# Two chained attention blocks on one core: the layer norm's statistics are aggregated on GpSimd instead of VectorE for later tiles, and six of the planner's numbers move

## The chip, the cores and the metric

The kernel runs on one core of one Trainium2 chip. The metric is the device time of one launch in microseconds (us), as the median of several runs. A core has five engines with instruction streams of their own: TensorE (PE, matmuls into PSUM), VectorE (DVE), ScalarE (ACT), GpSimd (POOL) and SyncE (SP, which here only issues DMAs). Each runs its stream in order; an instruction that needs another engine's result waits for a semaphore, and all that stands behind it on the same engine waits with it.

## The reference

The input x has 2048 rows of 512 numbers. Four layers follow each other, each on the layer norm of x and added back to x:

```python
x = x + _A_ref(_layernorm(x), wq, wk, wv, wo)    # layer 0: softmax attention, 32 heads of 16, one key/value head
x = x + _B_ref(_layernorm(x), wqkv, wo)          # layer 1: linear attention with phi(t) = t+1 or exp(t)
x = x + _A_ref(...)                              # layer 2, weights of layer 0
x = x + _B_ref(...)                              # layer 3, weights of layer 1
```

The layer norm takes, per row, the mean m and the variance v over 512 numbers and gives (x - m) / sqrt(v + 1e-5). The attention of a layer A needs 32 x 2048 x 2048 exponentials; that is the bulk of the kernel.

## The kernel before, in words

The rows are cut into 16 tiles of 128. Everything stays in SBUF; only the inputs come in and x goes out.

**The order is planned, not written.** A small list scheduler (class Planner, L36) is run while the kernel is built. Each operation is handed to `op` (L87) with the engines that may do it, a duration that the author gave it in us, a priority (low goes first), a latency until its result may be used, and what it reads and writes. The planner plays the engines forward in time and notes the order in which it gave work to each; `finalize` (L328) and `emit` (L351) then write one instruction stream per engine in that order with the waits that the data needs. What the planner thinks of durations thus decides only the order; on the chip each engine goes through its list and waits where the plan was too hopeful. GpSimd's own results are waited for by semaphore too, even on GpSimd.

**Layers A (`run_a`, L956).** The scores are cut into 4096 blocks of 128 keys by 512 (four heads-by-queries groups side by side) in the two A layers together. TensorE makes the scores of a block (L965). The exponential is then done in one of two ways. ScalarE takes two or three blocks in one activation (L1150). Or VectorE does one block: L1247 writes an integer whose bits, read as bfloat16, are about the exponential, and three shifted copies of four such blocks at a time (L1289) are made, so that the weighted sum of four shifted versions comes close to the true exponential; TensorE then multiplies four versions instead of one (L1019). Which block goes to which engine is decided while planning: VectorE gets a block when its queue of planned work is short (`dve_split`, `dve_open`, `alone`, L1231 to L1266, with the bounds BLS, BLO, BLT and DXB), and near the end of an attention only while more than ENDL blocks are left (L1201). VectorE starts on blocks only once the keys of tile 11 are planned (KGATE). L1312 and L1314 take the sums out of PSUM, L1334 to L1345 normalise them, `epilogue` (L1351) projects and adds to x.

**Filling TensorE.** When TensorE has nothing to do, `fill` (L1045) gives it matmuls with zeros (L1064), as many columns as a credit allows, which grows by WORK / 3.413 columns per us and falls by the columns run (`work`, L146).

**Layers B (`run_b`, L1413)** are short. Layer 1's tiles 0 to 14 are normalised and projected while layer 0's exponentials still run, as each tile's x is ready; so are layer 3's during layer 2. Only tile 15 and what depends on all of them come after. Layer 2's first tiles start when layer 1's first x tiles are there.

**The calm flag.** `pl.calm` is False while an attention's exponentials are planned (set at L1085) and True in the kernel's first moments and between the attentions (L692, L1168). Some rules hold in only one of the two: LAG (L64) holds back an operation in calm times when a more urgent one is about to come, HTOL (L72) lets a matmul go ahead of the next scores if it makes them late by no more than that.

**The layer norm of a tile (`ln_tile`, L787)** is what the change touches:

- L793, VectorE: bn_stats over the 512 numbers of each row. For even and odd elements apart it gives count, mean and sum of squared deviations: six numbers, tile st.
- L794, VectorE: bn_aggr makes mean and variance of them, tile mv.
- `slow_rs` (L781): L782 adds 1e-5 to the variance (on VectorE when the flag is calm or the tile is below 4 or from 12 on, else on GpSimd), and L784, on GpSimd, raises it to the power -0.5, tile rs. For the few critical tiles (tile 0 of layer 0, tiles 0 and 1 of layer 2, tile 15 of layers 1 and 3) ScalarE does it instead (L797, L798).
- L802, VectorE: (x - mean) * rs, tile xn, one of six buffers.
- Then xn is transposed into xnT, either by a DMA on SP's queue (L719) or on TensorE (L822) with a copy out of PSUM by ScalarE or VectorE (L827, recorded as L705). In layers 1 and 3 tiles below FARB take the DMA.

On VectorE, L802 has a priority that puts it behind L1247 of blocks but ahead of the shifts of L1289.

Of the kernel before, what the change touches and what calls it, by code (L numbers as in the profile page):

```python
# [7 lines left out]
FP32 = mybir.dt.float32  # L8
I16 = mybir.dt.int16
ACTF = mybir.ActivationFunctionType  # L10
ALU = mybir.AluOpType

PE, AC, DV, PO, SP = "pe", "act", "dve", "pool", "sp"
ENGS = (PE, AC, DV, PO, SP)

P = 128
S, D, H, DH = 2048, 512, 32, 16
T = S // P
# [388 lines left out]
NBQ = 3  # L407
LAG = 0.18
LAGP = 0.05
# [5 lines left out]
ECRIT = (15,)  # L415
WORK = 5500
RING = 24
# [5 lines left out]
FARA = (4, 4)  # L423
FARB = 12
FARO = 12
# [3 lines left out]
BLO = 5.0  # L429
DXB = 1.4  # L430
BLT = 2.5
# [14 lines left out]
SHIFT = 64.0  # L446
ENDL = 12
NSH = 4
# [31 lines left out]
ACRS = True  # L480
# [3 lines left out]
KSP = True  # L484
HTOL = 0.02
HK = 0.3
MCOP = (DV,)*4
EVP = 1.2
# [8 lines left out]
def bass_interleave_layers__grouped_kv_mqa__linear_attn_block__prompt_kernel(  # L497
# [35 lines left out]
    mv = sb("mv", [P, T, 2], FP32)  # L533
    ve = sb("ve", [P, T], FP32)
    zs = sb("zs", [P, 4], FP32)
    rs = sb("rs", [P, T], FP32)
# [244 lines left out]
    def slow_rs(t, prio, quick):  # L781
# [3 lines left out]
           reads=[("ve", t), "mhalf"], writes=[("rs", t)], prio=prio - 9.0)  # L785

    def ln_tile(t, prio, far=False, crit=False, dtl=None):  # L787
        if t in two:
            two.discard(t)
            n = 2  # L790
        else:
            n = 1
            op({DV: (0.6, lambda e: e.bn_stats(st[:, t, 0, :], x_sb[:, t, :]))}, reads=[("x", t)], writes=[("st", t)], prio=prio, lat=0.13)  # L793
        op({DV: (0.09, lambda e: e.bn_aggr(mv[:, t, :], st[:, t, 0:n, :]))}, reads=[("st", t)], writes=[("mv", t)], prio=prio, lat=0.13)  # L794
        quick = pl.calm or t < QUICK[0] or t >= QUICK[1]
        if crit and ACRS:
            op({AC: (0.2, lambda e: e.activation(ve[:, t:t + 1], mv[:, t, 1:2], ACTF.Ln, bias=eps5[:]))}, reads=[("mv", t), "eps5"], writes=[("ve", t)], prio=prio, lat=0.12)  # L797
            op({AC: (0.2, lambda e: e.activation(rs[:, t:t + 1], ve[:, t:t + 1], ACTF.Exp, scale=-0.5))}, reads=[("ve", t)], writes=[("rs", t)], prio=prio, lat=0.12)  # L798
        else:
            slow_rs(t, prio, quick)  # L800
        i = yield ("acq", xn_pool, prio)
        op({DV: (0.325, lambda e: e.tensor_scalar(out=xn[:, i, :], in0=x_sb[:, t, :], scalar1=mv[:, t, 0:1], scalar2=rs[:, t:t + 1],  # L802
                                                op0=ALU.subtract, op1=ALU.mult))},
           reads=[("x", t), ("mv", t), ("rs", t)], writes=[("xn", i)], prio=prio, port=True)
        if far:
# [1076 lines left out]
```

## Time and profile before

| | |
|---|---|
| median of 3 runs | 1488.83 us (1487.35 to 1489.05) |
| the profiled execution's own time | 1489.33 us |
| its span, first to last instruction | 1487.6 us |
| around the span | 1.7 us |
| granted TensorE clock, mean | 0.999 |
| instructions of the layer norm's statistics on VectorE (L793, L794) | 60 and 64 |

The page's first two parts, busy time by engine and the span in 40 slices (each digit a share in tenths):

```profile
PE 1433.2 (96%) x14825; PEld 520.1 (35%) x14924; DVE 1439.2 (97%) x2686; ACT 1452.5 (98%) x1444; POOL 77.0 (5%) x155
...
PE   8999999999999999999999999999999999999998
PEld 5423333333333333333733333333333333333335
DVE  8999999999999999999878999999999999999996
ACT  8999999999999999999799999999999999999996
POOL 5000000000000000000011000000000000000000
```

How to read it: PE's busy time counts the filler matmuls. A row of a group of instructions gives line, engine, operation, output and inputs, shape, count, then busy time and mean duration in ns, then the engine's idle time ahead of them. Rows of the timeline give start and duration in us, and in brackets the idle time before and what ended it. Rows of windows give the stretch, its length, and the busy time of PE, PEld, DVE, ACT and POOL, each with its number of instructions, then granted clock, share of the DMA engines and GB/s.

### The profile page before, as it was taken

The page shows a single profiled execution, that of the slowest core. Times are in us where ns is not written, and L with a number is a line of the kernel's source. Part 1 is how long each engine was busy: PE and PEld are TensorE (multiplying, and loading weights), DVE is VectorE, ACT ScalarE, POOL GpSimd, SP SyncE. Part 2 cuts the span into 40 slices and gives each one's busy share as a digit, 9 for nine tenths or more (in the row PEclk, how much of TensorE's full clock was granted, in tenths as well). Part 3 has the DMA queues.
Part 4 walks back from the last instruction along what each step waited for, and adds up shares of the span by engine and source line. Part 5 has one row for each costly group of instructions (what it writes and reads, how often), then busy time and mean ns, then how long its engine had stood idle before and what let it go on. Part 6 is the DMA issues. An engine that isn't in the chain of part 4 may idle for free.

```text
span 1487.6 us, 36547 instructions
## 1 busy us (share of the span) xinstructions
PE 1433.2 (96%) x14825; PEld 520.1 (35%) x14924; DVE 1439.2 (97%) x2686; ACT 1452.5 (98%) x1444; POOL 77.0 (5%) x155
## 2 busy tenths in 40 slices
PE   8999999999999999999999999999999999999998
PEld 5423333333333333333733333333333333333335
DVE  8999999999999999999878999999999999999996
ACT  8999999999999999999799999999999999999996
POOL 5000000000000000000011000000000000000000
PEclk9999999999999999999999999999999999999999
DMA  5200000000000000000031000000000000000001
GB/s 115 72 9 9 9 8 7 6 7 6 9 9 9 9 5 5 2 2 2 2 47 40 2 12 9 12 9 5 8 9 5 9 9 9 9 2 2 2 2 58
DMA packets 53542, 20.74 MB, mean 14 GB/s; under 512 B 47232, under 2 KB 52864, under 8 KB 53376
## 3 DMA queue, kind: packets, MB, share of 16 engines
q1 hardware_dynamic: 52320, 18.36, 5.7%
q8 instruction: 120, 1.97, 0.6%
q14 instruction: 46, 0.38, 0.1%
q10 hardware_dynamic: 1056, 0.03, 0.0%
HBM read 5.28 MB, written 2.10 MB: 5 GB/s over the span
## 4 chain that ended last, share of the span: by engine, by line
DVE 46%; PE 38%; ACT 7%; issue 7%; DMA 1%; POOL 0%; POOLq 0%; SPq 0%; ACTq 0%
DVE FB L1247 22%; DVE FB L1289 16%; PE ps L1019 13%; PE ps L965 11%; ACT PT L1150 7%; PE ps L711 5%; PE ps L1064 4%; PE ps L879 2%; PE ps L1334 1%; DVE sacc L1312 1%; DVE st L793 1%; DVE xn L802 1%; DVE QT L1422 1%; DVE Osb L1345 1%; DVE sacc L1422 1%
## 5 line engine op out<-in xcount | busy, mean ns | idle before, releaser
L1150 ACT ACTIVATE PT<-ps 128x1024 bf16<-128x1024 f32 (+1 forms) x1309 | 1400.1, 1309 | 5.6 <-PE ps L1019 2.7
L1247 DVE TENSOR_SCALAR FB<-ps 128x512 int16<-128x512 f32 x1047 | 689.0, 680 | 4.4 <-PE ps L965 3.1
L965 PE MATMUL ps<-QT,KM 32*128 32x512 bf16 x4096 | 525.6, 385 | 24.9 <-ACT PT L1150 16.9
L1019 PE MATMUL ps<-FB,VW 128*32 128x512 bf16 x4188 | 526.1, 384 | 8.3 <-DVE sacc L1312 5.3
L1289 DVE TENSOR_SCALAR FB<-FB 128x2048 int16<-128x2048 int16 (+1 forms) x789 | 517.6, 676 | 0.3
L1019 PE MATMUL ps<-PT,V 128*32 128x512 bf16 x3049 | 472.8, 386 | 0.4 <-issue 0.3
L965 PEld LDWEIGHTS ps<-QT,KM 32*128 32x128 bf16 x4096 | 133.0, 91 | 466.5 <-ACT PT L1150 381.7
L1064 PE MATMUL ps<-QT,V 128*32 128x512 bf16 (+6 forms) x927 | 249.8, 347 | 0.4
L1019 PEld LDWEIGHTS ps<-FB,VW 128*32 128x32 bf16 x4188 | 130.4, 94 | 163.3 <-issue 97.1
L1019 PEld LDWEIGHTS ps<-PT,V 128*32 128x32 bf16 x3049 | 114.7, 94 | 102.9 <-issue 74.5
L1064 PEld LDWEIGHTS ps<-QT,V 128*32 128x32 bf16 x927 | 79.8, 96 | 88.6 <-issue 32.9
L784 POOL TENSOR_TENSOR rs<-ve,mhalf 128x1 f32<-128x1 f32 x59 | 43.9, 745 | 578.9 <-DVE ve L782 576.6
L711 PE MATMUL ps<-wqkv,xnT 128*128 128x512 bf16 (+1 forms) x217 | 62.2, 367 | 7.0 <-issue 3.5
L1419 ACT ACTIVATE phE<-ps 128x512 bf16<-128x512 f32 (+1 forms) x66 | 45.8, 696 | 6.0 <-PE ps L879 5.0
L782 POOL TENSOR_SCALAR ve<-mv 128x1 f32<-128x1 f32 x32 | 14.9, 466 | 683.8 <-DVE mv L794 683.7
L1312 DVE COPY sacc<-ps 128x512 f32<-128x512 f32 x64 | 43.6, 681 | 3.3 <-PE ps L1019 3.2
L1334 PE MATMUL ps<-identF,sacc 128*128 128x128 f32 x256 | 46.3, 291 | 0.0
L793 DVE BATCH_NORM_STATS2 st<-x_sb 128x6 f32<-128x512 bf16 x60 | 40.5, 681 | 2.5 <-DMA x_sb<-in_A_x_dram 2.3
L879 PE MATMUL ps<-xnT,wqkv 128*128 128x128 bf16 x512 | 38.0, 220 | 0.0
L879 PE MATMUL ps<-xnT,wq 128*128 128x128 bf16 x464 | 35.2, 220 | 0.0
L1334 PEld LDWEIGHTS ps<-identF,sacc 128*128 128x128 f32 x256 | 27.3, 140 | 20.6 <-issue 11.8
L879 PEld LDWEIGHTS ps<-xnT,wqkv 128*128 128x128 bf16 x512 | 29.5, 98 | 9.8 <-issue 7.0
(139 smaller groups left out, 630.4 us busy)
## 6 DMA issues: line engine op xcount, KB each, us to landing
out_dram<-x_sb SPq DMA_DIRECT2D x16, 128.0 KB, 1.7
x_sb<-in_A_x_dram SPq DMA_DIRECT2D x6, 256.0 KB, 5.0
wqkv<-in_B_wqkv_dram SPq DMA_DIRECT2D x1, 1536.0 KB, 8.7
xnT<-xn SPq DMA_TRANSPOSE x48, 2.4
x_sb<-in_A_x_dram SPq DMA_DIRECT2D x4, 128.0 KB, 2.4
wq<-in_A_wq_dram SPq DMA_DIRECT2D x1, 512.0 KB, 4.5
wo<-in_A_wo_dram SPq DMA_DIRECT2D x1, 512.0 KB, 5.4
wo<-in_B_wo_dram SPq DMA_DIRECT2D x1, 512.0 KB, 9.4
```

The lines of the kernel that those rows point to most:

```text
L711: return e.matmul(dst, lhsT=l, rhs=r, start=(k == 0), stop=(k == len(pairs) - 1))
L793: op({DV: (0.6, lambda e: e.bn_stats(st[:, t, 0, :], x_sb[:, t, :]))}, reads=[("x", t)], writes=[("st", t)], prio=prio, lat=0.13)
L879: ins = e.matmul(dst[:, g * P:(g + 1) * P], lhsT=lhs(g, k), rhs=rhs(k), start=(k == 0), stop=(k == FT - 1))
L965: return e.matmul(bank(b), lhsT=KM[r, sg.par, kt * P:(kt + 1) * P], rhs=QT[r, sg.t, :], start=True, stop=True)
L1019: ins = e.matmul(ps[32 * j:32 * j + 32, ACC * 512:(ACC + 1) * 512], lhsT=V[:, kt, :] if w is None else VW[:, kt, w, :], rhs=ap, start=(k = ...
L1064: o = op({PE: (n / 2400.0, lambda e: e.matmul(ps[32 * j:32 * j + 32, b * 512:b * 512 + n], lhsT=V0[:], rhs=QT[:, sg.t, 0:n], start=st, sto ...
L1150: ex = op({AC: (EXO + 0.4267 * n, lambda e, n=n, s_=s_, p_=p_: e.activation(PT[:, p_, 0:n * 512], ps[:, s_ * 512:(s_ + n) * 512], ACTF.Exp ...
L1247: o = op({DV: (0.602, lambda e: e.tensor_scalar(out=dst.bitcast(I16), in0=bank(b), scalar1=VB, scalar2=VLO, op0=ALU.add, op1=ALU.max))}, w ...
L1289: o = op({en: (du, lambda e, w=w, g_=g_: e.tensor_scalar(out=FB[:, g_, 0:n].bitcast(I16), in0=FB[:, f_, 0:n].bitcast(I16), scalar1=float(w ...
L1312: o = op({DV: (0.6, lambda e, src=src: e.tensor_copy(src, bank(ACC)))}, writes=[B_(ACC), key], prio=0.0, lat=0.15)
L1334: o = op({PE: (0.12, lambda e, c=c: e.transpose(ps[:, b * 512 + c * P:b * 512 + (c + 1) * P], src[:, c * P:(c + 1) * P], identF[:]))}, rea ...
L1419: op({AC: (0.07 + n / 1200.0, lambda e: e.activation(phE[:, i, 0:n], bank(b, n), ACTF.Exp))}, reads=[B_(b)], writes=[("phE", i)], prio=pr ...
```

## The change

In `ln_tile`, tiles from 4 on (PAT) whose statistics come from one bn_stats over the whole row, which are not critical, and which come up while the calm flag is down, no longer run bn_aggr on VectorE. GpSimd makes mean and variance from the six numbers of bn_stats in four operations on one column (half the difference of the two means d, the mean of the two sums w, the mean of the two means, d * d + w), then adds 1e-5 in a fifth and raises to the power -0.5 as before. For tiles 12 and up this takes the add of 1e-5 from VectorE too. The planner is told 0.3 us (PAD) for each. A way to run L802 on GpSimd as well is written but off (PXN is False). Six numbers of the planner move: LAG, WORK, FARB, DXB, ENDL and HTOL.

```diff
-LAG = 0.18
+LAG = 0.15
...
-WORK = 5500
+WORK = 5000
...
-FARB = 12
+FARB = 11
...
-DXB = 1.4
+DXB = 1.6
...
-ENDL = 12
+ENDL = 14
...
-HTOL = 0.02
+HTOL = 0.05
 HK = 0.3
+PAT = 4
+PAD = 0.3
+PXN = False
...
+    dm = sb("dm", [P, T, 2], FP32)
...
+    def pool_rs(t, prio):
+        a, b = st[:, t, 0, 0:3], st[:, t, 0, 3:6]
+        d, w = dm[:, t, 0:1], dm[:, t, 1:2]
+
+        def po(out, in0, s1, s2, op0, op1, reads, writes):
+            op({PO: (PAD, lambda e: e.tensor_scalar(out=out, in0=in0, scalar1=s1, scalar2=s2, op0=op0, op1=op1))}, reads=reads, writes=writes, prio=prio - 9.0)
+        po(d, a[:, 1:2], b[:, 1:2], 0.5, ALU.subtract, ALU.mult, [("st", t)], [("dm", t)])
+        po(w, a[:, 2:3], b[:, 2:3], 1.0 / D, ALU.add, ALU.mult, [("st", t)], [("dw", t)])
+        po(mv[:, t, 0:1], a[:, 1:2], b[:, 1:2], 0.5, ALU.add, ALU.mult, [("st", t)], [("mv", t)])
+        po(ve[:, t:t + 1], d, d, w, ALU.mult, ALU.add, [("dm", t), ("dw", t)], [("ve", t)])
+        op({PO: (PAD, lambda e: e.tensor_scalar(out=ve[:, t:t + 1], in0=ve[:, t:t + 1], scalar1=1e-5, scalar2=None, op0=ALU.add))},
+           writes=[("ve", t)], prio=prio - 9.0)
+        op({PO: (0.55, lambda e: e.tensor_tensor(out=rs[:, t:t + 1], in0=ve[:, t:t + 1], in1=mhalf[:], op=ALU.pow))},
+           reads=[("ve", t), "mhalf"], writes=[("rs", t)], prio=prio - 9.0)
+
     def ln_tile(t, prio, far=False, crit=False, dtl=None):
...
-        op({DV: (0.09, lambda e: e.bn_aggr(mv[:, t, :], st[:, t, 0:n, :]))}, reads=[("st", t)], writes=[("mv", t)], prio=prio, lat=0.13)
+        slow = n == 1 and not pl.calm and not crit and t >= PAT
+        if not slow:
+            op({DV: (0.09, lambda e: e.bn_aggr(mv[:, t, :], st[:, t, 0:n, :]))}, reads=[("st", t)], writes=[("mv", t)], prio=prio, lat=0.13)
         quick = pl.calm or t < QUICK[0] or t >= QUICK[1]
-        if crit and ACRS:
+        if slow:
+            pool_rs(t, prio)
+        elif crit and ACRS:
...
-        op({DV: (0.325, lambda e: e.tensor_scalar(out=xn[:, i, :], in0=x_sb[:, t, :], scalar1=mv[:, t, 0:1], scalar2=rs[:, t:t + 1],
+        op({(PO if slow and PXN else DV): (0.7 if slow and PXN else 0.325, lambda e: e.tensor_scalar(out=xn[:, i, :], in0=x_sb[:, t, :], scalar1=mv[:, t, 0:1], scalar2=rs[:, t:t + 1],
                                                 op0=ALU.subtract, op1=ALU.mult))},
-           reads=[("x", t), ("mv", t), ("rs", t)], writes=[("xn", i)], prio=prio, port=True)
+           reads=[("x", t), ("mv", t), ("rs", t)], writes=[("xn", i)], prio=prio - 9.0 if slow and PXN else prio, port=True)
```

## Prediction

> **What bounds the kernel now.** The first view is the page: its costliest groups. The reader is to see that two engines share one job, the 4096 blocks (128x512) of exponentials: ScalarE does 3049 of them (the count of matmuls that read its tile PT), VectorE 1047 (the count of L1247), and each of VectorE's costs a further share of the 789 shift operations of L1289.
>
> ```profile
> span 1487.6 us, 36547 instructions
> ...
> L1150 ACT ACTIVATE PT<-ps 128x1024 bf16<-128x1024 f32 (+1 forms) x1309 | 1400.1, 1309 | 5.6 <-PE ps L1019 2.7
> L1247 DVE TENSOR_SCALAR FB<-ps 128x512 int16<-128x512 f32 x1047 | 689.0, 680 | 4.4 <-PE ps L965 3.1
> ...
> L1289 DVE TENSOR_SCALAR FB<-FB 128x2048 int16<-128x2048 int16 (+1 forms) x789 | 517.6, 676 | 0.3
> L1019 PE MATMUL ps<-PT,V 128*32 128x512 bf16 x3049 | 472.8, 386 | 0.4 <-issue 0.3
> ```
>
> The second view is the busy time by stage (columns: PE, weight loads, VectorE, ScalarE, GpSimd, then the granted TensorE clock). In the two attention stretches both engines are full: VectorE is idle 3.6 us of 662 and 2.8 us of 629, ScalarE 0.8 and 1.9. GpSimd is nearly empty there. In the start, the middle and the tail there are holes on both.
>
> ```profile
> 0.00:43.00 43.00, 38.09 (x397) 21.19 (x401) 33.93 (x104) 36.89 (x41) 21.85 (x71) 1.00 0.57 143
> 43.00:705.00 662.00, 640.21 (x6584) 211.75 (x6626) 658.39 (x1176) 661.23 (x637) 21.28 (x23) 1.00 0.03 7
> 705.00:816.00 111.00, 107.77 (x1101) 53.54 (x1108) 90.14 (x213) 98.92 (x118) 15.65 (x37) 0.98 0.17 30
> 816.00:1445.00 629.00, 608.69 (x6368) 209.72 (x6405) 626.24 (x1129) 627.10 (x614) 18.22 (x24) 1.00 0.04 7
> 1445.00:1488.00 43.00, 38.41 (x387) 23.93 (x389) 30.50 (x68) 28.34 (x38) 0.00 (x0) 1.00 0.15 50
> ```
>
> So the bound is ScalarE and VectorE together, and time freed on one is worth only its share. The third view, VectorE's timeline, gives VectorE's real price: durations overlap, and the step from one start to the next is 0.60 us where the duration says 0.68.
>
> ```profile
> 297.74 0.68 DVE L1247 TENSOR_SCALAR FB<-ps 128x512 int16<-128x512 f32 x1
> 298.34 0.68 DVE L1289 TENSOR_SCALAR FB<-FB 128x2048 int16<-128x2048 int16 x1
> 298.94 1.40 DVE L1247 TENSOR_SCALAR FB<-ps 128x512 int16<-128x512 f32 x2
> ```
>
> A block costs ScalarE 1400.1 / 3049 = 0.459 us and VectorE 0.60 + 789 x 0.60 / 1047 = 1.052 us. If the planner hands blocks over until both end together, 1 us freed on VectorE shortens a stretch by 0.459 / (0.459 + 1.052) = **0.304 us**. That is the exchange rate of every VectorE term below; without a hand-over it would be nothing.
>
> **The change part by part.** *Relief of VectorE.* The views of lines L794 and L782:
>
> ```profile
> L794 DVE BATCH_NORM_AGGREGATE mv<-st x64: 125/171/209, 3.8 to 1458.0; 128x2 f32<-128x6 f32 x60, 128x2 f32<-128x12 f32 x4
> L782 POOL TENSOR_SCALAR ve<-mv x32: 208/397/1172, 12.2 to 1295.8; 128x1 f32<-128x1 f32 x32
> L782 DVE TENSOR_SCALAR ve<-mv x27: 97/144/153, 7.2 to 1424.9; 128x1 f32<-128x1 f32 x27
> ```
>
> The 32 adds on GpSimd are tiles 4 to 11 of all four layers, so the "calm" flag is down for them in every layer, the first and third too. Tiles from 4 on then take the new path in layers 0 and 2 (12 each) and, without the critical tile 15, in layers 1 and 3 (11 each): 46 aggregates leave VectorE, and with them the 14 adds of tiles 12 and up (4 + 3 + 4 + 3 of the 27). The steps are in this stretch of VectorE's timeline: aggregate to next start 0.09 us, add to next start 0.06 us.
>
> ```profile
> 95.75 0.17 DVE L794 BATCH_NORM_AGGREGATE mv<-st 128x2 f32<-128x6 f32 x1
> 95.84 0.66 DVE L1289 TENSOR_SCALAR FB<-FB 128x2048 int16<-128x2048 int16 x1
> 96.42 0.14 DVE L782 TENSOR_SCALAR ve<-mv 128x1 f32<-128x1 f32 x1
> 96.48 1.28 DVE L1289 TENSOR_SCALAR FB<-FB 128x2048 int16<-128x2048 int16 x2
> ```
>
> 46 x 0.09 + 14 x 0.06 = 5.0 us of VectorE, at 0.304 = **-1.5 us**. Bounds: by full durations 46 x 0.171 + 14 x 0.144 = 9.9 us, so -3.0; counting only the 22 tiles inside the full stretches (22 x 0.09 + 6 x 0.06 = 2.3 us), -0.7.
>
> *GpSimd's chain and the instruction behind it.* GpSimd now runs five small operations and the power per tile: four more instructions for 32 tiles, five more for 14, 198 in all. The instruction that waits for the last is L802 on VectorE; VectorE runs in order, so every L1247 and L1289 behind it waits too, and ScalarE's partner work with them. How GpSimd fares against VectorE is seen at one tile (VectorE first, then GpSimd):
>
> ```profile
> 385.27 0.68 DVE L793 BATCH_NORM_STATS2 st<-x_sb 128x6 f32<-128x512 bf16 x1
> 385.87 0.67 DVE L1247 TENSOR_SCALAR FB<-ps 128x512 int16<-128x512 f32 x1
> 386.46 0.17 DVE L794 BATCH_NORM_AGGREGATE mv<-st 128x2 f32<-128x6 f32 x1
> 386.55 1.26 DVE L1289 TENSOR_SCALAR FB<-FB 128x2048 int16<-128x2048 int16 x2
> 387.75 0.69 DVE L1247 TENSOR_SCALAR FB<-ps 128x512 int16<-128x512 f32 x1
> 388.54 0.41 DVE L802 TENSOR_SCALAR xn<-x_sb,mv,rs 128x512 bf16<-128x512 bf16 x1
> ```
>
> ```profile
> 386.72 1.13 POOL L782 TENSOR_SCALAR ve<-mv 128x1 f32<-128x1 f32 x1 [40.22 <-DVE mv L794]
> 387.93 0.57 POOL L784 TENSOR_TENSOR rs<-ve,mhalf 128x1 f32<-128x1 f32 x1
> ```
>
> An add on one column takes 1.13 us here because it ends only 0.1 us after the second L1289; at the start, with no L1289 about, the same add takes 0.23 us and the next instruction starts 0.16 us after it:
>
> ```profile
> 12.24 0.23 POOL L782 TENSOR_SCALAR ve<-mv 128x1 f32<-128x1 f32 x1
> 12.40 0.19 POOL L682 MEMSET ones<- 1x128 bf16 x1
> ```
>
> And L802 started 0.04 us after the power's end (388.50), about 0.2 us later than the 0.60 step from 387.75 allows: VectorE already waits a little. Now the walk for the new path at this tile. The statistics end at 385.95; GpSimd starts about 386.03 and gets two operations done before the pair of L1289 (from 386.46, since the aggregate is gone, to 387.66); the third ends near 387.8, the square-and-add near 388.1, the add of 1e-5 near 388.3, the power 0.57 later: about 388.95, which is 3.0 us after the statistics. The planner allows 0.13 + 5 small operations of 0.30 with two gaps of 0.08, then 0.55 + 0.08: 2.42 us (before: 0.13 + 0.09 + 0.13 + 0.58 + 0.63 = 1.56). So L802 is placed some 0.9 us later than before and the chain ends some 0.4 us later, relative to it, than before. The wait added lies between 0 (other work placed ahead of L802) and 1.2 us (a tile with two L1289 in the chain's way). I take 0.2 us, near the wait the row shows today, for the 22 tiles inside the full stretches: 4.4 us less some 1.3 us of such waits that go (7 tiles like this one, an estimate), 3 us, at 0.304 = **+0.9 us** (bounds 0 and 22 x 1.2 x 0.304 = +8.0).
>
> Does GpSimd hold VectorE? At the tile of 297 us the power is stretched, not the L1289 at 298.34, which starts in the middle of it and keeps its 0.68 us:
>
> ```profile
> 297.33 0.57 POOL L782 TENSOR_SCALAR ve<-mv 128x1 f32<-128x1 f32 x1 [39.06 <-DVE mv L794]
> 297.99 1.07 POOL L784 TENSOR_TENSOR rs<-ve,mhalf 128x1 f32<-128x1 f32 x1
> ```
>
> So nothing is added for it. (The Trainium skill, "SBUF — State Buffer", section "SBUF: two separate sides", says the two engines share a port pair as an exclusive lock that goes to whichever starts first, the other blocking fully. By that rule the L1289 would have waited here; the trace agrees that one blocks the other, but not that the first comer wins.)
>
> *Start and middle.* 24 tiles of layers 0 and 2 get a chain longer by four or five steps of 0.16 to 0.23 us, 0.6 to 1.2 us. GpSimd has room (21.85 of 43 us busy; 12 tiles add 52 instructions, 8 to 12 us). These delays overlap from tile to tile, and what they feed is the keys before VectorE's first block. If they reach it in full, VectorE loses 1 us twice, +0.6; nothing if hidden. I take **+0.2**.
>
> *FARB 12 to 11.* Tile 11 of layers 1 and 3 is transposed on TensorE, with a copy, and not by DMA (48 transposes of xn become 46 on SP's queue, which frees nothing that the end waits for). The copy:
>
> ```profile
> L705 DVE COPY xnT<-ps 128x512 bf16<-128x512 bf16 x10 | 4.1, 410 | 1.1 <-PE ps L822 1.1
> ```
>
> Two copies of 0.41 less the 0.08 overlap, 0.7 us, at 0.304: **+0.2** (0 to +0.3).
>
> *The planner's other numbers.* DXB 1.4 to 1.6 lets a block start on VectorE with more work before it; VectorE's idle time in the two stretches is 6.4 us, and I let 40% of it be filled, at 0.304: **-0.8** (0 to -1.9). WORK 5500 to 5000 gives the filler matmuls of L1064 less credit, LAG and HTOL move the order of the calm phases and of TensorE, ENDL stops VectorE's blocks two earlier at the end. TensorE is not late for ScalarE in the stretches (5.6 us of idle time before 1309 exponentials), so I take **0**; but one clock dip shows what order can cost, in the middle stretch (first its window, then ScalarE's timeline after it):
>
> ```profile
> 750.00:755.00 5.00, 4.37 (x33) 1.60 (x33) 2.85 (x6) 4.64 (x5) 0.00 (x0) 0.78 0.38 79
> ```
>
> ```profile
> 755.29 2.36 ACT L1150 ACTIVATE PT<-ps 128x1536 bf16<-128x1536 f32 x2 [0.65 <-PE ps L965]
> 757.88 1.45 ACT L1150 ACTIVATE PT<-ps 128x1536 bf16<-128x1536 f32 x1 [0.22 <-PE ps L965]
> 759.92 1.02 ACT L1150 ACTIVATE PT<-ps 128x1024 bf16<-128x1024 f32 x1 [0.59 <-PE ps L1019]
> ```
>
> Each dip costs ScalarE up to 0.65 + 0.22 + 0.59 = 1.5 us, so one gone or one more is 1.5 us either way. A changed order also moves the hand-over at each attention's end by a block of VectorE, 1.05 us, twice: about 2 us either way.
>
> Sum: -1.5 + 0.9 + 0.2 + 0.2 - 0.8 = **-1.0 us**. The profiled execution took 1489.33 us (span 1487.6 and 1.7 around it), so 1488.3 for its like; it lies 0.5 us above the median 1488.83. I forecast the median: **1487.8 us**.
>
> **The rivals.** *B, faster: the order comes out well.* Relief nearly in full (-2.5), no added waits, VectorE's idle time filled (-1.5), the dip gone (-1.5), the start no later, the copies +0.2: -5.3, 1483.5. For it: GpSimd's idle time in the stretches, and a longer planned chain that gives L802 more cover. Against it: each item is an upper bound. *C, slower: L802 stands in VectorE's queue.* The chain passes pairs of L1289 at most tiles and VectorE waits 1.2 us at 22 tiles: 26 us, +8.0 with a relief of only 1.5 against it, 1495.3. It decides from a mean wait of (3 + 1.5) / 0.304 / 22 = 0.67 us. For it: L802 starts 0.04 us after the power today. Against it: the planner counts the longer chain. *D, more clock dips:* with less filler three more of them at 1.5 us, +4.5, 1493.3; against it, the clock is 1.00 in both stretches. *E, GpSimd holds VectorE:* 198 instructions x 0.22 us x the share of L1289 in VectorE's busy time (517.6 of 1439, 0.36) = 15.7 us, +4.8, 1493.6; the row at 297.99 speaks against it. (This is what the rule of the Trainium skill's "SBUF — State Buffer", named above, would make of it.) *F, the change doesn't do what it says:* the aggregates stay where the calm flag is up, or nothing is handed over: 1488.8.
>
> **How the numbers follow.** 0.2% is 3 us, about what a measurement of this kernel can tell from no change. A (the sum, within 1485.9 to 1491.8) has 0.40, F 0.03: within 0.2% together 0.43. B has 0.35, faster. C 0.15, D 0.05, E 0.02: slower 0.22. For 8 in 10 I leave out some 0.07 of B below 1480 and 0.10 of C, D and E above 1494: range 1480 to 1494; the likeliest case alone 1485.9 to 1491.8.
>
> **What would show it.** Relief: 18 aggregates and 13 adds left on VectorE, and a few more L1247 (5 us / 1.51 = 3 more). Chain: from the end of the statistics to the power's end some 3 us in the stretches, and idle time ahead of L802 of about 4 us in all; over 15 us there is C. Dips: the granted clock by stage. E: L1289 longer than 0.68 us beside GpSimd. I am wrong if the middle or the tail changes by over 2 us, which nothing above prices, or if ScalarE's instruction mix (two or three banks) shifts.

## The result and the profile after

The changed kernel takes 1492.54 us (median of 7 runs, 1490.99 to 1494.05) against 1489.05 us (7 runs, 1487.35 to 1489.53): ratio 1.0026, interval 1.0016 to 1.0036. It is slower by a quarter of a per cent, 3.5 us. The range held the time; the forecast, 1487.8, was on the wrong side. The slow end of the range stood there for the rivals C, D and E, none of which is what the runs show, so that it held is luck.

Within one kernel the times fall into steps by the mean granted TensorE clock. The traces show what a step is: a profiled execution with no dip of the clock is at 1.000 (e12, e13), one with a single dip like that at 750 us is at 0.999 (before, after). Before, over the 87 runs beside the experiments: median 1487.4 us at clock 1.000 (51 runs), 1488.8 at 0.999 (23), 1490.3 at 0.998 (9); the other 4 are at 0.997. After: 1491.2 at 1.000 (3 runs), 1492.5 at 0.999 (1), 1494.0 at 0.998 (3). At equal clock the change costs **3.8 us**, and since all executions at 1.000 of one kernel lie within about 0.1%, this is the finer comparison; "at full clock" below means it, always against 1487.4. (Of two experiments, e9 and e17, no profile is read: the profiled execution took over twice the usual time.)

The profiled execution took 1492.54 us, clock 0.999 as before. Its costliest groups and the rows the prediction used, from the page (L1173, L1270, L1312, L825, L815 and L803 are the L1150, L1247, L1289, L802, L794 and L784 of before; L796 and L801 are the new operations, and L715, L891, L902 and L988 are the L711, L868, L879 and L965 of before):

```profile
span 1490.8 us, 36214 instructions
...
PE 1403.1 (94%) x14661; PEld 511.3 (34%) x14756; DVE 1428.9 (96%) x2618; ACT 1457.8 (98%) x1447; POOL 144.5 (10%) x353
...
L1173 ACT ACTIVATE PT<-ps 128x1024 bf16<-128x1024 f32 (+1 forms) x1310 | 1400.3, 1221 | 4.3 <-PE ps L988 3.6
L1270 DVE TENSOR_SCALAR FB<-ps 128x512 int16<-128x512 f32 x1042 | 684.9, 681 | 6.2 <-PE ps L988 4.8
L1312 DVE TENSOR_SCALAR FB<-FB 128x2048 int16<-128x2048 int16 x786 | 514.9, 677 | 0.3
L1042 PE MATMUL ps<-PT,V 128*32 128x512 bf16 x3054 | 487.7, 386 | 14.1 <-ACT PT L1173 9.3
...
L796 POOL TENSOR_SCALAR dm<-st 128x1 f32<-128x1 f32 x92 | 30.7, 343 | 888.5 <-DVE st L812 887.0
```

GpSimd has 198 instructions more (155 to 353), as counted. VectorE was relieved, yet it does *fewer* blocks (1042, it was 1047), not the 3 more that were forecast: the time freed was not turned into work. The busy time by stage (columns as in the prediction):

```profile
0.00:43.00 43.00, 38.36 (x411) 22.00 (x414) 32.28 (x86) 37.19 (x41) 34.32 (x115) 1.00 0.44 101
43.00:705.00 662.00, 622.21 (x6469) 207.96 (x6509) 652.03 (x1152) 660.66 (x633) 39.80 (x78) 1.00 0.04 10
705.00:816.00 111.00, 106.97 (x1119) 54.20 (x1126) 87.25 (x195) 101.59 (x122) 31.51 (x89) 1.00 0.17 30
816.00:1445.00 629.00, 593.90 (x6246) 202.12 (x6286) 624.42 (x1116) 626.94 (x615) 38.85 (x71) 1.00 0.03 6
1445.00:1491.00 46.00, 41.68 (x430) 25.03 (x430) 32.95 (x72) 31.44 (x41) 0.00 (x0) 1.00 0.14 47
```

VectorE stands idle 10.0 us in the first attention's stretch (3.6 before) and 4.6 in the second's (2.8 before). About 1.2 us of the 4.6 belong to this execution's dip of the clock, which lies in this stretch (VectorE idle 1.00 of these 5 us and 0.18 of the next 5); before's, at 750 us, lies outside its window:

```profile
1325.00:1330.00 5.00, 4.52 (x36) 1.45 (x33) 4.00 (x9) 3.96 (x4) 0.00 (x0) 0.66 0.01 3
```

To see where the 3.2 us of span were lost I measured, on ScalarE's timeline, from the first to the last exponential of each attention: 699.7 us before and 703.0 after in the first, 719.6 and 719.9 in the second; before the first exponential 9.4 and 9.1, between the attentions 24.2 and 24.0, behind the last 34.7 and 34.8. Both dips lie in the second attention, so the comparison is fair. **The first attention lost 3.3 us; all else together nothing.** The same windows around its start, before and then after:

```profile
9.00:43.00 34.00, 31.68 (x324) 15.22 (x326) 30.06 (x87) 33.28 (x32) 18.33 (x47) 1.00 0.57 144
43.00:50.00 7.00, 6.99 (x91) 3.43 (x92) 6.71 (x12) 7.00 (x9) 0.00 (x0) 1.00 0.33 115
50.00:690.00 640.00, 618.97 (x6335) 203.32 (x6375) 636.72 (x1138) 639.23 (x613) 21.28 (x23) 1.00 0.03 6
690.00:705.00 15.00, 14.25 (x166) 5.01 (x167) 14.97 (x28) 15.00 (x17) 0.00 (x0) 1.00 0.00 1
```

```profile
9.00:43.00 34.00, 31.62 (x336) 16.03 (x337) 28.10 (x69) 33.27 (x32) 30.50 (x91) 1.00 0.41 88
43.00:50.00 7.00, 6.75 (x73) 3.36 (x71) 3.49 (x6) 7.00 (x8) 2.46 (x8) 1.00 0.98 361
50.00:690.00 640.00, 601.24 (x6246) 199.93 (x6283) 634.70 (x1123) 638.66 (x611) 37.34 (x70) 1.00 0.03 6
690.00:705.00 15.00, 14.22 (x158) 4.67 (x158) 13.84 (x25) 15.00 (x16) 0.00 (x0) 1.00 0.01 1
```

VectorE's third number tells it: its idle time grows by 2.0, 3.2, 2.0 and 1.1 us, 8.3 in all, 5.2 of it before 50 us. And GpSimd's fifth: 30.5 of the 34 us before 43 are busy. It is no longer an engine with room. Its timeline there shows one tile after another, six operations each, with gaps of 0.1 us at most (start, duration):

```profile
24.65 0.58 POOL L803 TENSOR_TENSOR rs<-ve,mhalf 128x1 f32<-128x1 f32 x1
25.21 0.27 POOL L796 TENSOR_SCALAR mv<-st 128x1 f32<-128x1 f32 x1
25.46 0.52 POOL L796 TENSOR_SCALAR ve<-dm 128x1 f32<-128x1 f32 x1
25.95 0.31 POOL L796 TENSOR_SCALAR dm<-st 128x1 f32<-128x1 f32 x1
26.34 0.22 POOL L801 TENSOR_SCALAR ve<-ve 128x1 f32<-128x1 f32 x1
26.65 0.26 POOL L796 TENSOR_SCALAR dm<-st 128x1 f32<-128x1 f32 x1
26.87 0.57 POOL L803 TENSOR_TENSOR rs<-ve,mhalf 128x1 f32<-128x1 f32 x1
```

From power to power 2.22 us. (The operations of two tiles are interleaved.) Twelve tiles pass through at this pace, and the tiles' scale comes out of GpSimd one by one. VectorE's timeline shows its first block before and after:

```profile
42.02 1.29 DVE L1247 TENSOR_SCALAR FB<-ps 128x512 int16<-128x512 f32 x2
```

```profile
31.80 0.41 DVE L825 TENSOR_SCALAR xn<-x_sb,mv,rs 128x512 bf16<-128x512 bf16 x1 [0.69 <-POOL rs L803]
...
46.54 1.54 DVE L891 TENSOR_SCALAR KM<-ps,kmask 128x512 bf16<-128x512 f32 x2 [1.88 <-PE ps L715]
48.00 0.68 DVE L1270 TENSOR_SCALAR FB<-ps 128x512 int16<-128x512 f32 x1
```

The first block is 6.0 us late: L825 waits 0.69 us for GpSimd, the transposes and projections behind it follow late (L715, 1.88 us), and the blocks open only with the keys of tile 11. This chain is read from the rows; that it alone makes the 6.0 us is not shown by them, and e2 below speaks against it.

### The profile page after: what moved, and what is told of

It reads as the page before. It is cut to its first block, busy times and chain, and to the rows that moved or that the text cites. A ratio compares the mean times of both kernels' runs of the same rounds, so it can differ in the third digit from the quotient of the medians.

```text
span 1490.8 us, 36214 instructions
## 1 busy us (share of the span) xinstructions
PE 1403.1 (94%) x14661; PEld 511.3 (34%) x14756; DVE 1428.9 (96%) x2618; ACT 1457.8 (98%) x1447; POOL 144.5 (10%) x353
## 4 chain that ended last, share of the span: by engine, by line
DVE 53%; PE 24%; ACT 13%; issue 5%; POOL 4%; DMA 0%; SPq 0%; POOLq 0%; ACTq 0%
DVE FB L1270 25%; DVE FB L1312 18%; ACT PT L1173 12%; PE ps L1042 8%; PE ps L988 7%; PE ps L715 3%; PE ps L1087 2%; PE ps L902 2%; DVE sacc L1335 2%; DVE st L812 1%; PE ps L1357 1%; DVE x_sb L1414 1%; DVE sacc L1445 1%; POOL rs L803 1%; POOL dm L796 1%
## 5 line engine op out<-in xcount | busy, mean ns | idle before, releaser
L1173 ACT ACTIVATE PT<-ps 128x1024 bf16<-128x1024 f32 (+1 forms) x1310 | 1400.3, 1221 | 4.3 <-PE ps L988 3.6
L1270 DVE TENSOR_SCALAR FB<-ps 128x512 int16<-128x512 f32 x1042 | 684.9, 681 | 6.2 <-PE ps L988 4.8
L1042 PE MATMUL ps<-FB,VW 128*32 128x512 bf16 x4168 | 541.5, 386 | 18.7 <-ACT PT L1173 10.5
L988 PE MATMUL ps<-QT,KM 32*128 32x512 bf16 x4096 | 529.0, 385 | 29.8 <-ACT PT L1173 20.4
L1312 DVE TENSOR_SCALAR FB<-FB 128x2048 int16<-128x2048 int16 x786 | 514.9, 677 | 0.3
L1042 PE MATMUL ps<-PT,V 128*32 128x512 bf16 x3054 | 487.7, 386 | 14.1 <-ACT PT L1173 9.3
L988 PEld LDWEIGHTS ps<-QT,KM 32*128 32x128 bf16 x4096 | 133.3, 91 | 437.5 <-ACT PT L1173 302.4
L1087 PE MATMUL ps<-QT,V 128*32 128x512 bf16 (+6 forms) x747 | 172.9, 309 | 1.8 <-DVE sacc L1335 0.7
L1042 PEld LDWEIGHTS ps<-PT,V 128*32 128x32 bf16 x3054 | 120.1, 94 | 127.5 <-issue 52.9
L796 POOL TENSOR_SCALAR dm<-st 128x1 f32<-128x1 f32 x92 | 30.7, 343 | 888.5 <-DVE st L812 887.0
L1087 PEld LDWEIGHTS ps<-QT,V 128*32 128x32 bf16 x747 | 59.6, 95 | 77.7 <-issue 49.3
L715 PE MATMUL ps<-wqkv,xnT 128*128 128x512 bf16 (+1 forms) x221 | 63.6, 367 | 7.7 <-issue 3.6
L1442 ACT ACTIVATE phE<-ps 128x512 bf16<-128x512 f32 (+1 forms) x66 | 41.3, 627 | 5.0 <-PE ps L902 3.9
L788 POOL TENSOR_TENSOR rs<-ve,mhalf 128x1 f32<-128x1 f32 x13 | 11.8, 909 | 303.6 <-DVE ve L786 296.5
L902 PE MATMUL ps<-xnT,wqkv 128*128 128x128 bf16 x512 | 37.8, 220 | 0.2
L825 DVE TENSOR_SCALAR xn<-x_sb,mv,rs 128x512 bf16<-128x512 bf16 x64 | 26.2, 411 | 11.7 <-POOL rs L803 8.8
L902 PE MATMUL ps<-xnT,wq 128*128 128x128 bf16 x464 | 35.4, 220 | 0.2 <-DVE FB L1270 0.2
```

The source lines that it names most:

```text
L715: return e.matmul(dst, lhsT=l, rhs=r, start=(k == 0), stop=(k == len(pairs) - 1))
L796: op({PO: (PAD, lambda e: e.tensor_scalar(out=out, in0=in0, scalar1=s1, scalar2=s2, op0=op0, op1=op1))}, reads=reads, writes=writes, prio= ...
L902: ins = e.matmul(dst[:, g * P:(g + 1) * P], lhsT=lhs(g, k), rhs=rhs(k), start=(k == 0), stop=(k == FT - 1))
L988: return e.matmul(bank(b), lhsT=KM[r, sg.par, kt * P:(kt + 1) * P], rhs=QT[r, sg.t, :], start=True, stop=True)
L1042: ins = e.matmul(ps[32 * j:32 * j + 32, ACC * 512:(ACC + 1) * 512], lhsT=V[:, kt, :] if w is None else VW[:, kt, w, :], rhs=ap, start=(k = ...
L1087: o = op({PE: (n / 2400.0, lambda e: e.matmul(ps[32 * j:32 * j + 32, b * 512:b * 512 + n], lhsT=V0[:], rhs=QT[:, sg.t, 0:n], start=st, sto ...
```

## The experiments

**First question: the chain or the six numbers?** e1 has the chain with the six old numbers; e2 has the new numbers without the chain; e3 and e4 have the new numbers and the chain in layers 1 and 3 only, or 0 and 2 only.

```diff
# e1: after, with
-LAG = 0.15  WORK = 5000  FARB = 11  DXB = 1.6  ENDL = 14  HTOL = 0.05
+LAG = 0.18  WORK = 5500  FARB = 12  DXB = 1.4  ENDL = 12  HTOL = 0.02
# e2: after, with
-PAT = 4
+PAT = 99
# e3 (e4): after; the one call of ln_tile in layers 0 and 2 (in layers 1 and 3) passes pat=99
-        slow = n == 1 and not pl.calm and not crit and t >= PAT
+        slow = n == 1 and not pl.calm and not crit and t >= pat
```

> The change's GpSimd chain with the six planner numbers left as they were before. Theory 1 (GpSimd paces the start of both softmax layers): the chain alone is slower than before, VectorE's first exponential block again starts near 48 us instead of 42.0 us, and the median lies 2.5 to 5 us above before. Theory 2 (the six numbers did the harm, by a worse order and more clock dips): within 1 us of before. Theory 3 (VectorE's wait ahead of the normalising instruction inside the full stretches): also slower, by 1 to 2 us, whatever the start does.

> The six planner numbers of the change without its GpSimd chain (the starting tile of the chain is set out of reach, so that every tile keeps the aggregate on VectorE). Theory 1: within 1 us of before or up to 2 us faster, first block near 42 us. Theory 2: 3 to 4 us slower than before, like the changed kernel. Theory 3: like theory 1.

> The changed kernel with the GpSimd chain in the linear-attention layers 1 and 3 alone, whose tiles come up inside the full stretches; layers 0 and 2 keep the aggregate on VectorE. Theory 1: the first block of each attention comes back to near 42 us and near 59 us after the second attention's first exponential, 3 to 4 us are won against the changed kernel, about the time of before. Theory 2: as slow as the changed kernel. Theory 3: still 1 to 2 us slower than before, since the waits of the 22 tiles in the stretches stay (some 4 us of VectorE).

> The changed kernel with the GpSimd chain in the softmax layers 0 and 2 alone, where it works during the start of each attention. Theory 1: as slow as the changed kernel, 2.5 to 4 us above before, first block near 48 us. Theory 2: the same as the changed kernel too, so this run is read beside e3. Theory 3: 1 to 2 us faster than the changed kernel.

Each was slower than before by about as much as the whole, or more: e1 1495.42 us (1.0042, 1.003 to 1.0054), e2 1493.23 (1.0034, 1.0023 to 1.0046), e3 1493.32 (1.004, 1.0026 to 1.0054), e4 1495.67 (1.0048, 1.0035 to 1.006). At full clock: +6.0 (2 runs), +3.8 (1 run), +4.8 (2), +5.9 (2). Parts that cost 6.0 and 3.8 alone and 3.8 together do not add up. But e2 has no work on GpSimd that before has not, and loses 3.8 us: so the six numbers, without the chain, can lose this much. The first blocks, on VectorE's timeline of e1, e2 and e4:

```profile
47.40 0.69 DVE L1270 TENSOR_SCALAR FB<-ps 128x512 int16<-128x512 f32 x1
```

```profile
45.83 0.68 DVE L1270 TENSOR_SCALAR FB<-ps 128x512 int16<-128x512 f32 x1
```

```profile
47.92 0.68 DVE L1270 TENSOR_SCALAR FB<-ps 128x512 int16<-128x512 f32 x1
```

e3's is at 45.8, as e2's. The chain in layer 0 makes it late (e4 against e2 and e3: some 2 us with the new numbers; e1 against before: 5.4 with the old), and the numbers make it late by 3.8 without the chain: VectorE waits for no power from 9 to 50 us in e2. So of the 6.0 us of the changed kernel the chain adds 2.2 to what the numbers cost already. The expectation of theory 1, that e3's block comes back to 42, failed.

**Second question: how much does a mere reordering cost?** Kernels with the instructions of before, but for the hand-over between the engines, where one planned duration is moved by a hair, so that the list scheduler falls into another order:

```diff
# e5, before, the planned duration of L1247
-            o = op({DV: (0.602,
+            o = op({DV: (0.603,
# e6, before
-EX_LAT = 0.185
+EX_LAT = 0.186
# e7, before, the planned duration of L794
-        op({DV: (0.09,
+        op({DV: (0.10,
```

> The kernel before with one planned duration moved by a hair: VectorE's block is planned at 0.603 us, not 0.602. The computation and the rules stay; only the list that the planner writes changes (most rows of VectorE's list move from the first hundred on). Theory P (the order of before is one favourable draw, and any other order costs some us): 3 to 6 us slower than before. Theory 1 (GpSimd in the start) and theory 3 (waits ahead of the normalising instruction): no GpSimd work is added, so within 1 us of before.

> The kernel before with the planned latency of an exponential at 0.186 us, not 0.185. Theory P: 3 to 6 us slower. Theories 1 and 3: within 1 us of before. Its list leaves that of before later than the other's, after some 400 rows of VectorE, so the start and the first block at 42.0 us stay; by theory P the first stretch is then longer after that point alone.

> The kernel before with the aggregate planned at 0.10 us, not 0.09. Theory P: 3 to 6 us slower, with the first block moved off 42.0 us, since the lists differ from row 35 on. Theories 1 and 3: within 1 us of before.

1491.66 (1.0031, 1.002 to 1.0042), 1492.16 (1.0028, 1.0017 to 1.0038) and 1490.77 us (1.0018, 1.0009 to 1.0026); at full clock **+3.9, +4.8 and +3.4** (5, 7 and 11 runs). Nothing that could cost was added. These orders lose in other places than the changed kernel: their first attention takes 698.6, 698.9 and 698.9 us, less than before's 699.7, and the first block is at 41.3 (e5), 41.4 and 42.9; the time between the attentions is 25.2, 28.6 and 26.2 us instead of 24.2, and the second attention 721.2, 719.0 and 719.8, without a dip (before's 719.6 holds one, worth about 1.4). The end of the first attention and the start of the second on ScalarE's timeline of e6:

```profile
698.95 8.98 ACT L1150 ACTIVATE PT<-ps 128x1024 bf16<-128x1024 f32 x8
...
736.51 6.88 ACT L1150 ACTIVATE PT<-ps 128x1024 bf16<-128x1024 f32 x6 [0.64 <-PE ps L965]
```

698.95 + 8.98 to 736.51 is 28.6 us. So before's order is a good one among its neighbours, and a rewrite that leaves it gave 3.4 to 4.8 us away here before its own merit counts (1.5 in e17, below).

**The same hair on the changed kernels, and single numbers.** e12 is after, e15 is e1 and e16 is e2, each with 0.603 as in e5; e17 and e18 are before with HTOL 0.05 alone and WORK 5000 alone; e8 is before with the chain in layers 1 and 3 and the old numbers.

> The changed kernel with VectorE's block planned at 0.603 us, not 0.602: another order of the changed kernel. Theory P: at undipped clock between 1490 and 1496 us, moved by up to 3 us from the changed kernel's 1491.2, either way. Theory 1: the first block again near 48 us, since GpSimd's load at the start stays, and the first attention again some 3 us longer than in the null orders of before (698.6 to 698.9 us from its first to its last exponential).

> The chain with the old six numbers (e1), and VectorE's block planned at 0.603 us: a second order with the chain. If the chain costs some 2 us beside the draw of the order, it lies at 1492 to 1496 us at full clock; if it costs nothing, near the orders without the chain, 1490.7 to 1492.2.

> The six numbers without the chain (e2), and VectorE's block planned at 0.603 us: a second order without the chain under the new numbers. If the chain costs some 2 us beside the draw, this lies at 1490 to 1492.5 us at full clock, under the two orders with both (1491.2 and 1494.7) on their mean; if the new numbers are the cost, at 1493 or more.

> The kernel before with HTOL at 0.05 alone (a matmul may make the next scores late by 0.05 us and not 0.02). Its lists differ from row 25 on. If HTOL is what puts the first block of the kernels with the new numbers at 45.8 us, it comes at 45 to 46.5 us here, and the first attention takes 701 to 703 us; if not, 41 to 43 us and 698.5 to 700 us. In both cases the time at full clock is 1490 to 1493 us, by theory P.

> The kernel before with WORK at 5000 alone (less credit for filler matmuls). Its lists differ from row 129 of VectorE on, inside the start. If WORK is what makes the first block late, it comes at 45 to 46.5 us here; if HTOL is, at 41 to 43 us. Time at full clock 1490 to 1493 us by theory P, and more runs below full clock than before if the filler kept TensorE's clock up.

> The kernel before with the GpSimd chain in layers 1 and 3 alone and the old six numbers: up to the first tile of layer 1 that takes the chain the order should be that of before, so the first block comes at 42.0 us. Theory 1: within 1 us of before or 0.7 us faster. Theory 3: waits of VectorE of some 4 us ahead of the normalising instruction, 0.5 to 1.5 us slower. Theory P: 3 to 6 us slower, and not by these waits.

| | median, us | ratio and interval | at full clock (runs) | first block, us | first attention, us |
|---|---|---|---|---|---|
| e12 | 1497.10 | 1.0058 (1.0045 to 1.007) | +7.3 (2 of 5) | 48.0 | 702.7 |
| e15 | 1494.32 | 1.0048 (1.0032 to 1.0063) | +5.8 (2 of 6) | 47.1 | 701.8 |
| e16 | 1493.79 | 1.0036 (1.0024 to 1.0048) | +5.4 (2 of 5) | 45.8 | 702.7 |
| e17 | 1488.93 | 1.0005 (0.9996 to 1.0014) | +1.5 (9 of 10) | not read | not read |
| e18 | 1494.99 | 1.0047 (1.0033 to 1.0061) | none (0 of 5) | 41.5 | 700.4 |
| e8 | 1496.92 | 1.0064 (1.005 to 1.0078) | +8.5 (3 of 6) | disturbed by a clock dip | disturbed |

Two of these missed what was expected: e17's +1.5 is below every range, and e8's +8.5, the largest loss of a freely planned order, is above them and stays open. e16, 1492.8 at full clock, falls between its two cases.

Three things follow. First, orders freely planned, with the chain in all four layers (after, e1, e12, e15), are at +3.8 to +7.3, mean +5.7; without it (e2, e5, e6, e7, e16, e17) at +1.5 to +5.4, mean +3.8. With the numbers kept equal the means differ by 1.0 us under the new ones (after, e12 against e2, e16) and by 1.9 under the old (e1, e15 against e5 to e7). A cost of the chain of 1 to 2 us is suggested and not settled, since the first two groups spread by 4 us each.

Second, a late first block goes with a long first attention: the free orders that have the block at 45.8 us or later (after, e1, e3, e4, e12, e15, e16) have first attentions of 700.6 to 703.0 us, mean 702.1; those with it at 41.3 to 42.9 (before, e5, e6, e7, e18) 698.6 to 700.4, mean 699.3. That is 2.8 us for 5.3 us of delay on the mean (47.1 against 41.8). All of the late ones have the chain or the new numbers, so this is a comparison of groups and not of the block's start alone; e2 is left out, since a dip of 6.8 us lies in its first attention. The chain is not needed for the loss: e16, the new numbers without it, takes 702.7 us, as long as e12 (702.7) and nearly as after (703.0), while the chain with the old numbers takes 700.6 and 701.8 (e1, e15) and mere reorderings 698.6 to 698.9. And the second attention shows no such price: after's first block there comes 64.1 us behind the first exponential, before's 58.9, and the attention is 0.3 us longer.

Third, dips come more often in some of these kernels than in others: of those with the new numbers 12 of 33 runs came at full clock, of e18, WORK alone, none of 5, of before 51 of 87. That less filler is the reason is not shown: with the old numbers and the chain it is 7 of 17 (e1, e8, e15), and of e5 to e7 23 of 27.

**Third question: what do the edits cost when the order stays?** In e9 to e11 the plan of before is made as it is, and only then, in the finished lists, aggregate and add are taken from VectorE's list and the five operations put directly ahead of the power in GpSimd's: in e9 for all tiles of the change, in e10 for those of layers 1 and 3, in e11 for those of layers 0 and 2. In e13, e10 has L802 of tiles 4 to 11 three places later in VectorE's list. In e14 the aggregates of layers 1 and 3 are left out and nothing replaces them (its output is not the reference's), so it shows the relief alone.

```diff
# e9 to e11, behind the planning (o of L794 is ag, of L782 ad, of L784 pw)
+            pl.order[ag.eng].remove(ag)
+            pl.order[ad.eng].remove(ad)
+            i = pl.order[PO].index(pw)
+            pl.order[PO][i:i] = [od, ow, om, ov_, oe]
# e13, besides
+        for o in later:
+            i = pl.order[DV].index(o)
+            pl.order[DV].insert(i + LATER, pl.order[DV].pop(i))
# e14, instead
+    for o in gone:
+        pl.order[DV].remove(o)
```

> The order of before held fixed: the planner runs as before, and after it the 46 aggregates and 14 adds are taken out of VectorE's list, and the five GpSimd instructions are put in front of each tile's power; every other instruction keeps its place on its engine. So the order can't change, and no block can be handed over. Theory P (the loss of the change is a less favourable order): within 1 us of before. Theory 1 (GpSimd paces the start): the first block some 3 to 6 us late and 1.5 to 4 us slower. Theory 3 (waits ahead of the normalising instruction): VectorE waits some 10 to 15 us more there and loses 2 to 5 us.

> As the last, the swap in layers 1 and 3 alone (22 aggregates and 6 adds): the tiles inside the full stretches. Theory P: within 0.7 us of before. Theory 1: the same, within 0.7 us. Theory 3: the chain ends 1 to 2 us after the place that the plan of before gave the normalising instruction, so 22 waits of some 0.5 to 1.5 us, 2 to 5 us slower.

> As e9, the swap in layers 0 and 2 alone (24 aggregates and 8 adds). Theory P: within 0.7 us of before. Theory 1: nearly all of e9's loss, 1.5 to 4 us, with GpSimd busy without a break from 12 to 40 us. Theory 3: under 1 us.

> As e10 (order of before held, swap in layers 1 and 3), but the normalising instruction of tiles 4 to 11 stands three places later in VectorE's list, some 1.8 us, so that GpSimd's chain is done before VectorE comes to it. Theory 3 (the loss of e10, 2.9 us at full clock, is VectorE's wait ahead of that instruction): the waits of those 16 tiles go, those of tiles 12 to 14 stay, and the time comes back to 1487.5 to 1488.5 us at full clock. If e10 lost by something else (GpSimd holding VectorE's shifts, say), it stays near 1490.2.

> The order of before held, and only the relief: the 22 aggregates of tiles 4 and up are left out in layers 1 and 3 and nothing is put in their place (those tiles are normalised with the mean and variance that the layer before left in the buffer, so the output is not the reference's). The sum of the prediction: 22 x 0.09 us at 0.304 is -0.6 us where blocks can be handed over; here they can't, so between 0 and -2 us. By theory P it stays within 0.7 us of before, since the order is kept.

e14: 1488.92 us (1.0003, 0.9994 to 1.0012), at full clock 1487.4, **0.0** (5 runs): about 2 us taken from VectorE (22 x 0.09) are worth nothing while the order is held. e10: 1490.54 (1.0018, 1.0009 to 1.0027), at full clock +2.8 (6 runs). e13: 1489.04 (1.0011, 1.0002 to 1.002), at full clock +1.45 (7 runs). Since e14 excludes the removal, e10's 2.8 us are the chain's, within the 2 to 5 that theory 3 expected; e13 gives back half of it by the place of L802 alone, less than expected (1488.5 us or below; it is 1488.8). The waits for GpSimd ahead of L802 by the view of waits (us in all, times, longest), before, e10 and e13:

```profile
DVE xn L802 <- POOL rs L784: 1.8, 3, 1.0
```

```profile
DVE xn L837 <- POOL rs L787: 5.9, 8, 1.1
```

```profile
DVE xn L844 <- POOL rs L789: 3.7, 5, 1.1
```

4.1 us more of wait cost 2.8, and 1.9 more cost 1.45: about 0.7 us for each, where the exchange rate says 0.304. In these two kernels a late VectorE is paid for at more than twice the rate, and in e14 an early one earns nothing. That the waits alone make the 2.8 us is argued from these two points.

e11: 1499.19 (1.0074, 1.0062 to 1.0087), no run at full clock; e9 1500.0 to 1504.1 in its other four executions (ratio 1.0096, 1.0083 to 1.011). Both are far above the 1.5 to 4 us that theory 1 expected. In e11's windows the start is the place:

```profile
0.00:43.00 43.00, 34.14 (x316) 18.61 (x317) 27.65 (x75) 30.98 (x34) 33.24 (x116) 0.91 0.43 95
```

GpSimd is busy 33.24 us instead of 21.85, ScalarE 30.98 instead of 36.89, TensorE 34.14 instead of 38.09, and the granted clock falls to 0.91; VectorE's first block comes at 50.9. ScalarE waits 8.2 us for scores in this start, 0.3 in before's; in the changed kernel, whose planner counts the longer chain, ScalarE keeps its work there (37.19 us) and only VectorE is late. How much of e11's time is the clock and how much the waiting is not told apart.

## Why the prediction was wrong, point by point

- **The sum's frame failed first.** It let the rest of the order stand and gave a changed order "about 2 us either way". Reorderings that change nothing else cost 3.4 to 4.8 us (e5 to e7), all to one side; all other free orders lie above before's too, so the order they leave is a favourable one. This term was left out of the -1.0, and it alone is of the size of the result.
- **The planner's other numbers, put at 0 beside DXB, failed with it.** Without the chain the six numbers cost 3.8 and 5.4 us at full clock (e2, 1 run; e16, 2 runs), and e16 loses 3.0 us in the first attention, where the change loses 3.3. The reason given for 0, that TensorE is not late for ScalarE in the stretches, did not cover VectorE's first block, 3.8 us late in e2. Whether this is the numbers or once more the reordering is not told apart, and neither is which number: WORK alone leaves the block at 41.5 (e18), HTOL alone costs 1.5 us (e17).
- **"Start and middle", +0.2, failed.** "GpSimd has room (21.85 of 43 us busy ...)" was read over a stage that begins 11 us before the tiles come. The added load was forecast (8 to 12 us; it is 34.32 - 21.85 = 12.5); what failed is "These delays overlap from tile to tile". After, GpSimd is busy for 30.5 of the 34 us from 9 to 43, the 12 tiles' delays queue behind each other at 2.2 us a tile, and the first block came 6.0 us later, not up to 1.2, of which 3.8 are there without the chain (e2). At the exchange rate 6.0 us are 6.0 x 0.304 = 1.8 us; the comparison by first block suggests up to 2.8, the second attention nearly nothing. In the first attention VectorE's idle time grew by 8.3 us, less 2.6 us that aggregates and adds took less: 5.7 x 0.304 = 1.7 of the 3.3 us lost there. The other 1.6 us are open.
- **Relief, -1.5, failed in its worth, not its size.** The 46 aggregates went (18 are left, as said; the next row), and aggregates and adds take 2.6 us less of VectorE in the first attention and 3.0 less in the second (each counted as its step to the next start, or as its duration where that is shorter), 5.6 for the 5.0 of the forecast. But the hand-over did not come: 5 blocks fewer instead of 3 more (mere reorderings have 3 to 7 fewer as well: 1043, 1044 and 1040 in e5 to e7), and e14 shows 0.0 in a fixed order.

```profile
L815 DVE BATCH_NORM_AGGREGATE mv<-st x18: 163/173/209, 4.0 to 1461.2; 128x2 f32<-128x6 f32 x14, 128x2 f32<-128x12 f32 x4
```

- **The wait ahead of L802, +0.9, was right in size where it was priced.** Over the whole kernel it is 8.8 us in 18 waits, first row below; in the stretches from 50 to 700 and from 816 to 1445 us it is 2.3 and 1.8, next to the 4.4 that were forecast; the other 4.7 are in the start and the middle. The tile at 386 us shows it: from the first operation's start to the power's end 385.16 to 388.11, 2.95 us (forecast 3.0), and a wait of 0.61. Rival C, which decides from 15 us, did not happen. That a wait can cost 0.7 instead of 0.304 (e10, e13) was not foreseen.

```profile
DVE xn L825 <- POOL rs L803: 8.8, 18, 0.8
```

```profile
385.16 1.22 POOL L796 TENSOR_SCALAR mv<-st 128x1 f32<-128x1 f32 x1
386.37 0.78 POOL L796 TENSOR_SCALAR ve<-dm 128x1 f32<-128x1 f32 x1
387.24 0.22 POOL L801 TENSOR_SCALAR ve<-ve 128x1 f32<-128x1 f32 x1
387.54 0.57 POOL L803 TENSOR_TENSOR rs<-ve,mhalf 128x1 f32<-128x1 f32 x1
```

```profile
385.66 1.28 DVE L1312 TENSOR_SCALAR FB<-FB 128x2048 int16<-128x2048 int16 x2
386.86 0.68 DVE L1270 TENSOR_SCALAR FB<-ps 128x512 int16<-128x512 f32 x1
388.15 0.41 DVE L825 TENSOR_SCALAR xn<-x_sb,mv,rs 128x512 bf16<-128x512 bf16 x1 [0.61 <-POOL rs L803]
```

- **Rival E fell.** L1312 takes 677 ns on the mean; by the trace the 72 of 786 that have a GpSimd operation beside them take 680, the others 676. At 385.16 it is again GpSimd's operation that is stretched, to 1.22 us, though it began first. (The rule of the Trainium skill's "SBUF — State Buffer", section "SBUF: two separate sides", that the first comer holds the port, would have stretched L1312; with these one-column operations no kept trace shows that: no shift that started inside one takes over 0.71 us.) GpSimd can hold VectorE, though, with a wider operation: in nine kernels (e2 to e8, e12, e16) one shift that starts inside GpSimd's 128x128 multiply takes 0.88 to 0.89 us; five others that do (after, e1, e16, two in e18) keep 0.68 or 0.69. In e5 the pair of shifts beside it takes 1.49 us instead of 1.28, and the multiply 0.78 instead of 0.40:

```profile
819.51 1.49 DVE L1289 TENSOR_SCALAR FB<-FB 128x2048 int16<-128x2048 int16 x2
```

```profile
819.67 0.78 POOL L849 TENSOR_TENSOR VW<-V,wts 128x128 bf16<-128x128 bf16 x1 [6.03 <-DVE V L705]
```

- **DXB, -0.8:** VectorE's idle time was not filled: it grew by 6.4 us in the first stretch, and by 1.8 in the second, 1.2 of them in the dip. No kernel here has DXB alone, so its own share is open.
- **Rival D and the filler, 0:** both profiled executions have one dip, and the 3.8 us are measured at full clock, so D is not their cause. But dips were more frequent in the kernels with the new numbers (12 of 33 runs at full clock against 51 of 87), at about 1.4 us each, in the medians.
- **Rivals B and F:** B's gains did not come. Of F the second half did, on balance nothing was handed over, but the price was not nothing.
- **"I am wrong if the middle or the tail changes":** they did not (24.2 to 24.0 and 34.7 to 34.8 us), and ScalarE's mix did not shift (878 and 431 instructions of two and three banks, 876 and 434 after), so these signs did not catch the error. With the old numbers, or WORK alone moved, free orders other than before's have middles of 25.2 to 28.6 us (e1, e5 to e7, e15, e18); with the new ones 24.0 to 24.8 (after, e2 to e4, e12, e16). So the orders under the new numbers have the shorter middle and the longer first attention.

In short: that GpSimd is full in the start and passes one tile per 2.2 us is shown, and so is that mere reorderings cost as much as the change (e5 to e7) and that the six numbers do without the chain (e2, e16). That the late chain is what the change lost by is not shown: e16 loses nearly as much in the first attention without it, and in e11 the chain's waits are mixed with a lower clock. How the 3.8 us divide between the chain's own cost (1 to 2 us on the mean) and the luck of the order is not settled. None of these kernels beat before.

## What to carry to other kernels

Where a planner makes the order, first move a planned number by a hair and time that: the loss it shows (here 3.4 to 4.8 us) is the noise below which no edit can be judged, and it need not be centred on zero (all other free orders here lay above before's). Run the retuned numbers without the edit too (e2, e16): here they lost as much alone. Then put the edit into the finished lists with the order held, once as a whole and once only what it removes (e10, e14); and compare executions of equal granted clock. Read an engine's room in the window in which the work arrives, not over the stage, and by the pace of one item (2.2 us a tile), not by its sum.

## What the runs showed of the hardware

An operation on a single column takes GpSimd 0.22 to 0.31 us in most rows at 25 us, 0.52 for the square-and-add and 0.57 for the power, but 0.78 and 1.22 beside a pair of L1312; the shifts keep 0.68 us beside them (680 ns against 676). Six such operations hold a tile for 2.2 us, where VectorE's aggregate and add step on in 0.09 and 0.06 us. A 128x128 multiply on GpSimd that began first stretched one shift to 0.88 or 0.89 us in nine kernels, and left 0.68 or 0.69 in five other pairs. A single dip of the granted clock costs about 1.4 us here, and whether it comes differs from one execution of the same program to the next.
